# A new opening for a linear-attention and gated-MLP kernel: the first four token tiles are centred before they are transposed, and normalised at the exit of V

## The chip, the cores and the metric

The kernel runs on one core of a Trainium2 chip. Its time is the device time of one execution in microseconds (us), as the median of several runs. A profile is the record of one such execution: every instruction with its engine, start and length, the waits between engines, and the packets of the transfers. The engines are PE (matrix multiply, with PEld for its weight loads), DVE (vector), ACT (activation functions), POOL (general purpose) and SP, which in this kernel does nothing but issue transfers (DMAs).

## The reference

One layer norm of `x` (2048 tokens, 640 features) feeds two branches, whose outputs are added to `x`. Branch A is linear attention with 32 heads of 20 features; its feature map is a softmax of plus and of minus the mapped vector. Branch B is a gated MLP of width 1536.

```
xn  = (x - mean) / sqrt(var + 1e-5)
q, k, v = split(xn @ wqkv)                      # per head: 2048 x 20
phi(a)  = concat(softmax(a @ w_phi), softmax(-(a @ w_phi)))
kv  = sum over s of phi(k)[s, f] * v[s, d];   z = sum over s of phi(k)[s, f]
A   = ((phi(q) @ kv) / (phi(q) . z + 1e-6)) @ wo
B   = (silu(xn @ w1) * (xn @ w3)) @ w2
out = x + A + B
```

All inputs and the output are bfloat16.

## The kernel before

The 2048 tokens are 16 tiles of 128, the 640 features 5 chunks of 128. The kernel is written as a list of operations; a planner inside it (`schedule`, lines 166 to 370) gives each operation a planned start, picks the engine where an operation may run on two, and so fixes the order of the instructions on each engine. `emit` then turns each dependence into a semaphore wait. All engines work through their own lists in order; an instruction that waits holds back everything behind it on its engine. All transfers are issued by SP, in one list. Loads and stores go through line 606, transfers that transpose (called turns here) through line 612. All matmuls but the fillers and the transposes are recorded by line 544, all instructions of DVE, ACT and POOL by line 552, so groups are told apart by their tiles.

What happens in the opening, by its names:

- `load_x` brings tiles of `x` into `x_tok`: tiles 0, 1, 2, 3 alone, then 4 to 7, 8 to 11 and 12 to 15 together. `wv` (the V columns of wqkv) comes in two halves of 320 columns, `phi_s` holds w_phi, `load_wT` turns the K part of wqkv into `wqkT` in five pieces (and later the Q part), `load_w13` brings column ranges of w1 and w3 (512 columns of each at a time).
- `ln_stats` computes mean and variance of a tile on DVE (two statistics and one aggregate) and 1/sqrt(var + eps) on POOL into `mv[:, t, 4]`. `ln_apply` normalises the tile in place, on DVE, or from tile 4 on also on ACT.
- Tiles 0 to 3 are transposed on PE (`xn_transpose`, against `ident`) into `xnT`, the transposed normalised input. Tiles 4 to 15 are turned into `xnT` by a DMA each (`turn`), which SP issues once the tile is normalised.
- `v_half` and `v_tile` multiply a tile of `xnT` by `wv` into `v2`, which keeps a column of ones beside each head. `fold(1, dc)` multiplies `wqkT` by a block diagonal `BDc` of w_phi, so that `Wkp` is w_k times w_phi; `fold(0, dc)` does the same for Q into `Wqp`. `k_tile` multiplies by `Wkp` and takes the exponentials of plus and minus the result (`ekt`); `k_norm` sums and scales them (DVE and POOL).
- `mlp(b, fc)` is one MLP unit: 10 matmuls of 512 tokens (5 by w1, 5 by w3), a tanh on ACT into `th`, two steps on DVE into `t1` and `hT`.
- `filler` gives PE matmuls on zeros in the first 12 planned us where it would be idle.
- `consts_fold` makes the mask `GF` that `block_diag` needs on POOL, `consts_late` the masks `GK`, `PT` and `epsc` and `ones_late` the ones in `v2`.

Then come, with MLP units between them, V and K of tiles 4 to 15, the sum over tokens (`kv_sum`, `kv_back`), Q (`q_proj`), the attention output of each tile (`q_tok`, whose result `o_tok` is turned into `oT`), and the output tiles (`out_tile`: 12 chunks of w2 and 5 of wo, then the sum with `x` from `xres`, and the store).

The planner's main rules that the change touches: a transfer ends 1.35 us after its bytes at 330 GB/s behind those before it; among operations of one engine that can start within 0.03 us of the earliest, the one with the highest level goes first; dependences are kept by regions of 32 bytes (`GRAN`), and an overwrite of what the same engine has read needs no wait, except on POOL.

Of the kernel before, what the change touches and what calls it, by code (L numbers as in the profile page):

```python
# [9 lines left out]
D = 640  # L10
# [10 lines left out]
ENGINES = ("PE", "ACT", "DVE", "POOL", "SP")  # L21
SEM = {"PE": 0.06, "ACT": 0.04, "DVE": 0.04, "POOL": 0.08, "SP": 0.05}
MODE = 0.097
GRAN = 32
BACKLOG = 2.5


# [4 lines left out]
class _Op:  # L32


    __slots__ = ("ways", "eng", "emit", "raw", "war", "bankd", "succ", "unit", "ismm", "start", "end", "inc", "sem",
                 "clock", "idx", "part", "level", "off", "done", "nbytes", "busy", "left", "name", "deps", "gates")

    def __init__(self, ways):
        self.ways = ways
        self.eng = next(iter(ways)) if len(ways) == 1 else None  # L40
        self.raw, self.war, self.bankd, self.succ = set(), set(), set(), []
        self.unit = None
        self.ismm = self.inc = self.part = self.done = False
        self.sem = None
        self.nbytes = 0
        self.level = 0.0
        self.off = 0.0
        self.name = ""
        self.gates = []


class _Unit:
# [11 lines left out]
class _Program:  # L64
# [101 lines left out]
    def schedule(self, start, filler=None, filler_until=0.0):  # L166
# [45 lines left out]
        def commit(o, e, t):  # L212
            nonlocal bus, pool_prev
            o.eng = e
            o.emit, o.busy, dur = o.ways[e]
            o.start = t
            free[e] = t + o.busy
            if o.nbytes:
                bus = max(bus, t + 0.6) + o.nbytes / 330e3
                o.end = bus + 1.35  # L220
            else:
                o.end = t + dur
            o.done = True
# [66 lines left out]
        while left:  # L290
            best = None
            pick = None
            if ready_u:
                t0 = free["PE"]
                blocked = set()
                cands = []
                for u in ready_u:
                    extra = MODE if u.mode != mode else 0.0
                    u.at = max(unit_time(u), t0 + extra)
                for u in sorted(ready_u, key=lambda u: (-u.level, u.mms[0].idx)):  # L300
                    opts = []
                    for k in range(0, 8, u.banks):
                        if blocked & set(range(k, k + u.banks)):
                            continue
                        g = group_time(u, k)
                        if g < 1e8:
                            opts.append((max(g, u.at), fit(k, u.banks, u.at), k))
                    if opts:
                        x = min(opts)
                        if pick is None or x[0] < pick[0] - (0.03 + MODE):  # L310
                            pick = (x[0], u, x[2])
                    if u.banks == 4 and u.at <= t0 + 1.0 and not blocked and (not opts or x[0] > u.at + 0.03):
                        k = min((group_time(u, k, True), k) for k in (0, 4))[1]
                        blocked |= set(range(k, k + 4))
                if pick is not None:
                    best = (pick[0], "PE", pick[1], pick[2])
            for e in ("ACT", "DVE", "POOL", "SP"):
                if not ready[e]:
                    continue
                ts = [(max(free[e], op_time(o, e)), o) for o in ready[e]]  # L320
                t = min(x[0] for x in ts)
                t, o = min((x for x in ts if x[0] <= t + 0.03), key=lambda x: (-x[1].level, x[1].idx))
                if best is None or t < best[0]:
                    best = (t, e, o, None)
            assert best is not None, [(len(ready_u), {e: len(r) for e, r in ready.items()})]
            t, e, x, k = best
            if e == "PE":
# [44 lines left out]
    def emit(self, finish):  # L372
# [55 lines left out]
def bass_parallel_sum__linear_kernel_hedgehog__glu_gated_swiglu__prompt_kernel(  # L428
# [52 lines left out]
    th = new("th", [128, 3, 512], f32)  # L481
    t1 = new("t1", [128, 3, 512], bf)
    xres = new("xres", [128, 4, D], bf)

    RX = region(20480)
    x_tok = new("x_tok", [128, T, D], bf, RX)
# [60 lines left out]
    def way(eng, name, args, kw, busy, lat):  # L547
# [2 lines left out]

        def emit():
            return getattr(e, name)(*[at(a, u) for a in args], **{k: at(v, u) for k, v in kw.items()})  # L552
        return eng, (emit, busy, lat)

    def sb(*aps):
        return [a for a in aps if hasattr(a, "ap")]
# [51 lines left out]
    def turn(o, i, level=0.0, dram=False):  # L608
        n = 2
        for s in o.shape:  # L610
            n *= s
        return P.dma("SP", lambda: nc.sync.dma_start_transpose(o, i), sb(o), sb(i), n,  # L612
                     1.3 * n / 163840, level)

# [13 lines left out]

    def load_wT(which, e, level):
        turn(wqkT[:, which * DC + e:which * DC + e + 1, :],
             A_wqkv[:, which * D + 128 * e:which * D + 128 * e + 128], level)

# [41 lines left out]
    def ln_stats(t0, n, level):  # L676
        for t in range(t0, t0 + n):
# [5 lines left out]
        m, v, r, z = mv[:, t0:t0 + n, 0], mv[:, t0:t0 + n, 1], mv[:, t0:t0 + n, 4], mv[:, t0:t0 + n, 5]  # L683
        add([w_op("POOL", "tensor_scalar_add", (r, v, EPS), 0.21, 0.25)], [r], [v], None, level)
        add([w_op("POOL", "tensor_tensor", (r, r, mhalf[:, 0:n], ALU.pow), 0.55 + 0.1 * (n - 1),
                  0.6 + 0.1 * (n - 1))], [r], [r, mhalf[:, 0:n]], None, level)
# [2 lines left out]
            add([w_op("POOL", "tensor_tensor", (z, z, r, ALU.mult), 0.21, 0.25)], [z], [z, r], None, level)  # L689

    def ln_apply(t, level):
        o, m, s, z = x_tok[:, t, :], mv[:, t, 0:1], mv[:, t, 4:5], mv[:, t, 5:6]
# [3 lines left out]
        add(ways, [o], [o, m, s, z] if t >= 4 else [o, m, s], None, level)  # L696

    def xn_transpose(t, level):
        u = P.begin(1, level)
# [266 lines left out]
    load_w13(0, 512, lv - 20)  # L966
    load_x(8, 12, lv - 21)
    load_w13(512, 1024, lv - 22)
    load_x(12, 16, lv - 23)
# [1 line left out]
    for e in range(DC):  # L971
        load_wT(0, e, lv - 30 - e)

    consts_fold()
    for t in range(4):
        ln_stats(t, 1, 1e5 - t)
        ln_apply(t, 2e5 - t)
    block_diag(0)
    for t in range(4):
        xn_transpose(t, 5e4 - 10 * t + 15)  # L980
    for t in range(4, T, 2):
        ln_stats(t, 2, 1e5 - t)
        ln_apply(t, 2e5 - t)
# [105 lines left out]
```

## Time and profile before

| | us |
|---|---|
| four runs | 278.53, 277.63, 277.31, 278.11 |
| median | 277.87 |
| the profiled execution, its own time | 278.53 |
| its span, from first to last instruction | 276.8 |

The profiled execution is the first of the four; its span leaves out 1.7 us that lie around the instructions. The granted clock of PE was 1.00.

The first 17 us, busy time of each engine (PE's includes 37 matmuls on zeros):

| PE | PEld | DVE | ACT | POOL |
|---|---|---|---|---|
| 13.92 | 8.63 | 8.05 | 6.71 | 10.04 |

A row of the timeline gives start, length, engine, line, operation, tile written and tiles read, shapes and count, and in brackets the idle time before it and what ended it. A length of several instructions runs from the first's start to the last's end, and a matmul's end is some 0.17 us after the next one's start, because they are pipelined: steps between starts are what one costs. A row of the chain of waits gives start, length and what the end of the kernel hung on in that time.

### The profile page before, as it was taken

What the parts mean: (1) busy time and instruction counts of PE and PEld (TensorE: products, weight loads), DVE (VectorE), ACT (ScalarE), POOL (GpSimd) and SP (SyncE); (2) the same over time, 40 slices, a digit from 0 to 9 for tenths busy, and PEclk for the clock granted to TensorE, in tenths of its full rate; (3) what the DMA queues carried; (4) which work ended last, traced back from release to release, by engine and by line L of the source; (5) the groups of instructions that cost most, each with busy time, mean ns of one, the idle gap of its engine ahead of it and who ended that gap; (6) DMA issues with size and microseconds to landing.
All of it is one profiled execution on the core that took longest, in us unless ns stands there. A gap on an engine that the chain in (4) does not pass through costs nothing.

```text
span 276.8 us, 5029 instructions
## 1 busy us (share of the span) xinstructions
PE 268.4 (97%) x2076; PEld 158.9 (57%) x2097; DVE 177.5 (64%) x311; ACT 101.8 (37%) x188; POOL 60.5 (22%) x101
## 2 busy tenths in 40 slices
PE   7899999999999999999999999999999999999996
PEld 3575565666664446644444445767777775444774
DVE  3667899998756444478968979667761215566212
ACT  2478577456445441247573383010000001322000
POOL 7712548999459000000000000000000000000000
PEclk9999999999999999999999999999999999999999
DMA  7899997840000000801211121233332222000001
GB/s 209 130 343 243 247 190 146 153 153 0 2 0 0 2 0 2 266 22 26 46 27 24 24 50 24 73 94 100 96 90 78 73 71 73 0 0 0 26 24 47
DMA packets 40583, 21.98 MB, mean 79 GB/s; under 512 B 26992, under 2 KB 40560, under 8 KB 40560
## 3 DMA queue, kind: packets, MB, share of 16 engines
q1 hardware_dynamic: 40560, 21.66, 32.5%
q8 instruction: 16, 0.26, 0.4%
q14 instruction: 7, 0.06, 0.1%
HBM read 12.81 MB, written 2.62 MB: 56 GB/s over the span
## 4 chain that ended last, share of the span: by engine, by line
PE 85%; DMA 5%; SPq 4%; DVE 2%; ACT 2%; issue 2%; POOL 1%
PE PS L544 85%; SPq L612 3%; DMA xnT<-x_tok 3%; DMA x_tok<-in_A_x_dram 2%; ACT EqT L552 2%; SPq L606 1%; DVE bst L552 1%; POOL mv L552 1%; DVE hT L552 0%; DVE den_s L552 0%; DVE xres L552 0%; ACT e_s L552 0%; DVE x_tok L552 0%; DVE mv L552 0%; DVE pr_s L552 0%
## 5 line engine op out<-in xcount | busy, mean ns | idle before, releaser
L544 PE MATMUL PS<-xnT,w_s 128*128 128x512 bf16 x463 | 105.9, 379 | 1.7 <-issue 0.5
L544 PEld LDWEIGHTS PS<-xnT,w_s 128*128 128x128 bf16 x480 | 46.3, 98 | 54.2 <-DVE hT L552 1.0
L544 PE MATMUL PS<-w_s,hT 128*128 128x320 bf16 x384 | 55.0, 299 | 0.0
L552 ACT ACTIVATE th<-PS 128x512 f32<-128x512 f32 x48 | 28.8, 599 | 64.1 <-PE PS L544 63.9
L552 DVE SCALAR_TENSOR_TENSOR t<-th,PS 128x512 bf16<-128x512 f32 x48 | 32.5, 677 | 22.9 <-ACT th L552 22.9
L544 PEld LDWEIGHTS PS<-w_s,hT 128*128 128x128 bf16 x384 | 37.1, 98 | 14.9
L552 POOL TENSOR_TENSOR ekt<-ekt,rS 128x640 bf16<-128x640 bf16 x32 | 39.6, 1271 | 11.1 <-DVE rS L552 11.1
L552 DVE TENSOR_TENSOR xres<-PS,xres 128x640 bf16<-128x640 f32 (+1 forms) x17 | 13.4, 786 | 41.2 <-PE PS L544 41.2
L552 DVE SCALAR_TENSOR_TENSOR hT<-t,PS 128x512 bf16<-128x512 bf16 x48 | 32.4, 675 | 1.4 <-PE PS L544 0.4
L552 ACT ACTIVATE EqT<-PS 128x512 bf16<-128x512 f32 x40 | 21.7, 594 | 12.5 <-PE PS L544 12.5
L552 DVE TENSOR_REDUCE S<-ekt 128x64 f32<-128x1280 bf16 x16 | 23.3, 1474 | 4.2 <-ACT ekt L552 4.1
L544 PE MATMUL PS<-wv,xnT 128*128 128x320 bf16 x160 | 24.9, 299 | 0.6 <-DMA xnT<-x_tok 0.6
L544 PE MATMUL PS<-wo_s,oT 128*128 128x320 bf16 x160 | 24.5, 299 | 0.0
L552 DVE TENSOR_TENSOR prod<-PS,g_s 128x1280 bf16<-128x1280 f32 x16 | 23.9, 1491 | 0.5
L544 PE MATMUL PS<-Wkp,xnT 128*128 128x320 bf16 x160 | 24.0, 299 | 0.0
L544 PE MATMUL PS<-xnT,Wqp 128*128 128x512 bf16 x96 | 23.1, 380 | 0.3 <-issue 0.2
L552 ACT ACTIVATE ekt<-PS 128x640 bf16<-128x640 f32 x32 | 20.5, 705 | 6.9 <-PE PS L544 6.8
L552 ACT ACTIVATE e_s<-PS 128x64 f32<-128x64 f32 x32 | 9.1, 284 | 37.8 <-PE PS L544 37.3
L544 PEld LDWEIGHTS PS<-wv,xnT 128*128 128x128 bf16 x160 | 15.2, 98 | 8.1 <-DVE hT L552 1.1
L552 DVE BATCH_NORM_STATS2 bst<-x_tok 128x6 f32<-128x320 bf16 x32 | 14.2, 478 | 7.7 <-DMA x_tok<-in_A_x_dram 7.6
L544 PEld LDWEIGHTS PS<-wo_s,oT 128*128 128x128 bf16 x160 | 15.7, 98 | 6.1
L544 PEld LDWEIGHTS PS<-Wkp,xnT 128*128 128x128 bf16 x160 | 15.5, 98 | 6.1 <-DVE hT L552 0.3
(58 smaller groups left out, 150.3 us busy)
## 6 DMA issues: line engine op xcount, KB each, us to landing
w_s<-in_B_w_dram SPq DMA_DIRECT2D x6, 640.0 KB, 9.0
xres<-in_A_x_dram SPq DMA_DIRECT2D x16, 160.0 KB, 2.2
out_dram<-xres SPq DMA_DIRECT2D x15, 160.0 KB, 1.8
x_tok<-in_A_x_dram SPq DMA_DIRECT2D x3, 640.0 KB, 5.8
w_s<-in_B_w_dram SPq DMA_DIRECT2D x1, 1920.0 KB, 9.3
wv<-in_A_wqkv_dram SPq DMA_DIRECT2D x2, 400.0 KB, 4.6
wo_s<-in_A_wo_dram SPq DMA_DIRECT2D x1, 800.0 KB, 6.1
x_tok<-in_A_x_dram SPq DMA_DIRECT2D x4, 160.0 KB, 4.6
```

Of the source, the lines that this page charges most:

```text
L544: return nc.tensor.matmul(o(u.k), l, r, start=start, stop=stop, skip_group_check=shared)
L552: return getattr(e, name)(*[at(a, u) for a in args], **{k: at(v, u) for k, v in kw.items()})
L606: return P.dma(eng, lambda: queue[eng].dma_start(o, i), sb(o), sb(i), n, 0.45, level, after)
L612: return P.dma("SP", lambda: nc.sync.dma_start_transpose(o, i), sb(o), sb(i), n, 1.3 * n / 163840, level)
```

## The change

It has five parts.

1. *The first four tiles.* ACT makes the negative mean of the tile (a copy scaled by -1/640 with an accumulated sum, `junk` takes the copy), DVE or ACT adds it to the tile (`centre`, into `xc`), PE transposes the centred tile (`xc_transpose`, into `xcT`; tile 0 in two parts), and `v_first` computes V from `xcT`, scaling by 1/sqrt(var + eps) as V leaves PSUM. The statistics, the normalisation in place and the transposes into `xnT` are still made for these tiles, since K, Q and the MLP use them; they follow.
2. *Transfers.* Tiles 0, 1 and 2 come first, then `wv` as five pieces of 128 rows, then tile 3, `phi_s`, the first 256 columns of w1 and of w3, the five `wqkT` turns, tiles 4 to 7, the next 256 columns of w1 and w3, and the rest as before.
3. *The planner's figures.* A transfer ends 1.2 us after its bytes, a turn from DRAM 1.0 and one from SBUF 0.2 later; operations can be given an earliest start; `block_diag` is not planned before 8 us, the late masks and ones not before 30.
4. *The planner's choices.* The highest level goes first among operations that can start within 0.09 us; an operation of high level is taken off an engine if another would end it sooner.
5. *Dependences.* Regions of 8 bytes; an overwrite of what the same engine has read now waits for it on all engines but PE.

```diff
-GRAN = 32
+GRAN = 8
...
-                o.end = bus + 1.35
+                o.end = bus + 1.2 + o.extra
...
-            t = 0.0
+            t = o.early
...
-                t = max(t, d.end + SEM[e] if d.eng != e or e == "POOL" or d.nbytes or o.nbytes else d.start)
+                t = max(t, d.end + SEM[e])
...
-                t, o = min((x for x in ts if x[0] <= t + 0.03), key=lambda x: (-x[1].level, x[1].idx))
+                t, o = min((x for x in ts if x[0] <= t + 0.09), key=lambda x: (-x[1].level, x[1].idx))
+                if len(o.ways) > 1 and o.level > 1.5e6:
+                    other = min(max(free[f], op_time(o, f)) + o.ways[f][2] for f in o.ways if f != e)
+                    if other < t + o.ways[e][2] - 0.02:
+                        ready[e].remove(o)
+                        del o.ways[e]
+                        moved = True
+                        continue
...
-                if d.eng == e and e != "POOL" and not d.nbytes and not o.nbytes:
+                if d.eng == e == "PE":
                     continue
...
+    def centre(t, level):
+        o, i, z = xc[:, t, :], x_tok[:, t, :], mv[:, t, 6:7]
+        add([way("ACT", "activation", (junk[:], i, ACT.Copy), dict(scale=-1.0 / D, accum_out=z), 0.8, 0.9)],
+            [junk[:], z], [i], None, level)
+        add([w_op("DVE", "tensor_scalar", (o, i, z, None, ALU.add), 0.35, 0.44), w_act(o, i, ACT.Identity, D, 1.0, z)],
+            [o], [i, z], None, level)
...
+    def xc_transpose(t, level):
+        n = 2 if t == 0 else 1
+        u = P.begin(n, level)
...
+    def v_first(t, level):
+        P.begin(2, level, stream="V").name = f"V{t}"
+        for i in range(DC):
+            for q in range(2):
+                mm(q, lambda k, q=q: bank(k + q, 320), xcT[:, t, i, :], wv[:, i, 320 * q:320 * q + 320],
+                   i == 0, i == DC - 1)
...
+        add([w_act(o, src, ACT.Copy, D, r), w_op("DVE", "tensor_scalar", (o, src, r, None, ALU.mult), 0.74, 0.83)],
+            [v2[:, t, 0:672]], [r], [0, 1], 1e6)
...
     load_x(0, 1, lv)
-    for q in range(2):
-        load(wv[:, :, 320 * q:320 * q + 320], wqkv_t[:, :, 2 * D + 320 * q:2 * D + 320 * q + 320], lv - 2 - 2 * q,
-             )
-        load_x(q + 1, q + 2, lv - 3 - 2 * q)
-    load_x(3, 4, lv - 6)
-    load(phi_s[:], phi_t, lv - 7)
+    load_x(1, 2, lv - 1)
+    load_x(2, 3, lv - 2)
+    for c in range(DC):
+        load(wv[:, c, :], wqkv_t[:, c, 2 * D:3 * D], lv - 3 - c)
+    load_x(3, 4, lv - 8)
+    load(phi_s[:], phi_t, lv - 9)
+    load_w13(0, 256, lv - 10)
     for e in range(DC):
-        load_wT(1, e, lv - 8 - e)
+        load_wT(1, e, lv - 12 - e)
     load_x(4, 8, lv - 19)
-    load_w13(0, 512, lv - 20)
+    load_w13(256, 512, lv - 20)
...
+    up = 2e6
+    for t in range(4):
+        ln_stats(t, 1, 2e5 - 10 * t)
     consts_fold()
+    n = len(P.all)
+    block_diag(0)
+    late(n, 8.0)
     for t in range(4):
-        ln_stats(t, 1, 1e5 - t)
-        ln_apply(t, 2e5 - t)
-    block_diag(0)
+        centre(t, up - t)
+        ln_apply(t, 1e5 - t)
     for t in range(4):
-        xn_transpose(t, 5e4 - 10 * t + 15)
+        xc_transpose(t, 6e4 - 10 * t + 15)
+    for t in range(4):
+        xn_transpose(t, 3e4 - t)
...
     for t in range(4):
-        for q in range(2):
-            v_half(t, q, 5e4 - 10 * t - q)
+        v_first(t, 6e4 - 10 * t)
...
+    n = len(P.all)
     consts_late()
     ones_late()
+    late(n, 30.0)
```

As the planner orders the changed program, PE's list in the opening is: 10 fillers, the transposes of centred tile 0, 4 fillers, those of tile 1, V of tile 0, the transposes of tile 2, V of tile 1, the transposes of tile 3, V of tiles 2 and 3, the four sets of transposes of normalised tiles, one MLP unit, three folds, one MLP unit, two folds, one MLP unit, K of tiles 0 to 3, one MLP unit, then V and K of tiles 4 to 8. SP's list after tiles 4 to 7 is: w1 and w3 (256 columns each), tiles 8 to 11, w1 and w3, tiles 12 to 15, w1, the turns of tiles 4 and 5, w3, one `wqkT` turn, the turns of tiles 6 and 7, one `wqkT` turn, the turns of tiles 8 and 9.

More of the change, by code (lines that the diff above doesn't have):

```diff
@@ L35 @@
     __slots__ = ("ways", "eng", "emit", "raw", "war", "bankd", "succ", "unit", "ismm", "start", "end", "inc", "sem",
-                 "clock", "idx", "part", "level", "off", "done", "nbytes", "busy", "left", "name", "deps", "gates")
+                 "clock", "idx", "part", "level", "off", "done", "nbytes", "busy", "left", "name", "deps", "gates", "early", "extra")
     def __init__(self, ways):
@@ L49, in __init__ @@
         self.gates = []
+        self.early = 0.0
+        self.extra = 0.0
 class _Unit:
@@ L316, in schedule @@
                     best = (pick[0], "PE", pick[1], pick[2])
+            moved = False
             for e in ("ACT", "DVE", "POOL", "SP"):
@@ L321, in schedule @@
                 t = min(x[0] for x in ts)
-                t, o = min((x for x in ts if x[0] <= t + 0.03), key=lambda x: (-x[1].level, x[1].idx))
+                t, o = min((x for x in ts if x[0] <= t + 0.09), key=lambda x: (-x[1].level, x[1].idx))
[6 more added lines that the diff above has]
+                        continue
                 if best is None or t < best[0]:
                     best = (t, e, o, None)
+            if moved:
+                continue
             assert best is not None, [(len(ready_u), {e: len(r) for e, r in ready.items()})]
@@ L483, in bass_parallel_sum__linear_kernel_hedgehog__glu_gated_swiglu__prompt_kernel @@
     xres = new("xres", [128, 4, D], bf)
+    xcT = P.sbuf("xcT", [128, 4, DC, 128], bf, P.base[xres[:].name])
+    xc = P.sbuf("xc", [128, 4, D], bf, P.base[th[:].name])
+    junk = P.sbuf("junk", [128, D], bf, P.base[t1[:].name])
     RX = region(20480)
@@ L552, in emit, with late @@
             return getattr(e, name)(*[at(a, u) for a in args], **{k: at(v, u) for k, v in kw.items()})
+        emit.__name__ = name
         return eng, (emit, busy, lat)
+    def late(first, us):
+        for o in P.all[first:]:
+            o.early = us
     def sb(*aps):
@@ L611, in turn @@
             n *= s
-        return P.dma("SP", lambda: nc.sync.dma_start_transpose(o, i), sb(o), sb(i), n,
-                     1.3 * n / 163840, level)
+        d = P.dma("SP", lambda: nc.sync.dma_start_transpose(o, i), sb(o), sb(i), n, 1.3 * n / 163840, level)
+        d.extra = 1.0 if dram else 0.2
+        return d
     x_t = A_x.rearrange("b (t p) d -> p (b t) d", p=128)
@@ L632, in load_wT @@
         turn(wqkT[:, which * DC + e:which * DC + e + 1, :],
-             A_wqkv[:, which * D + 128 * e:which * D + 128 * e + 128], level)
+             A_wqkv[:, which * D + 128 * e:which * D + 128 * e + 128], level, True)
     zeroed = []
@@ L682, in ln_stats @@
             add([w_op("DVE", "bn_aggr", (o, i), 0.13, 0.21)], [o], [i], None, level)
-        m, v, r, z = mv[:, t0:t0 + n, 0], mv[:, t0:t0 + n, 1], mv[:, t0:t0 + n, 4], mv[:, t0:t0 + n, 5]
+        m, v, r, z = mv[:, t0:t0 + n, 0], mv[:, t0:t0 + n, 1], mv[:, t0:t0 + n, 4], mv[:, t0:t0 + n, 6]
         add([w_op("POOL", "tensor_scalar_add", (r, v, EPS), 0.21, 0.25)], [r], [v], None, level)
@@ L691, in ln_apply @@
     def ln_apply(t, level):
-        o, m, s, z = x_tok[:, t, :], mv[:, t, 0:1], mv[:, t, 4:5], mv[:, t, 5:6]
+        o, m, s, z = x_tok[:, t, :], mv[:, t, 0:1], mv[:, t, 4:5], mv[:, t, 6:7]
         ways = [w_op("DVE", "tensor_scalar", (o, o, m, s, ALU.subtract, ALU.mult), 0.35, 0.44)]
@@ L696, in ln_apply, with emit, src @@
         add(ways, [o], [o, m, s, z] if t >= 4 else [o, m, s], None, level)
+    def centre(t, level):
[7 more added lines that the diff above has]
+        u = P.begin(n, level)
+        u.name = f"cT{t}"
+        for dc in range(DC):
+            l = xc[:, t, 128 * dc:128 * dc + 128]
+            j, b = (0, dc) if n == 1 or dc < 3 else (1, dc - 3)
+            def emit(l=l, j=j, b=b):
+                a = (u.k + j) * 1024 + 128 * b
+                return nc.tensor.transpose(PSb[:, a:a + 128], l, ident[:])
+            P.mm(emit, [l, ident[:]], j, 0.056, 128)
+        for j, a, b in ((0, 0, DC),) if n == 1 else ((0, 0, 3), (1, 3, DC)):
+            def src(k, j=j, n=b - a):
+                return PSb[:, (k + j) * 1024:(k + j) * 1024 + 128 * n].rearrange("p (c n) -> p c n", n=128)
+            o = xcT[:, t, a:b, :]
+            add([w_act(o, src, ACT.Copy, 128 * (b - a)), w_copy(o, src, 128 * (b - a), 2)], [o], [], [j], 1e6)
+    def v_first(t, level):
[4 more added lines that the diff above has]
+                   i == 0, i == DC - 1)
+        o = v2[:, t, 0:672].rearrange("p (b h c) -> p b h c", b=2, c=21)[:, :, :, 0:DH]
+        r = mv[:, t, 4:5]
+        def src(k):
+            return bank2(k, 320).rearrange("p b (h c) -> p b h c", c=DH)
+        add([w_act(o, src, ACT.Copy, D, r), w_op("DVE", "tensor_scalar", (o, src, r, None, ALU.mult), 0.74, 0.83)],
+            [v2[:, t, 0:672]], [r], [0, 1], 1e6)
     def xn_transpose(t, level):
```

## The prediction

> **What bounds the kernel now.** I read the shares of busy time first, then the chain that ended last, then TensorE's (PE's) own waits, then the first 30 us in order of time.
>
> ```profile
> span 276.8 us, 5029 instructions
> ...
> PE 268.4 (97%) x2076; PEld 158.9 (57%) x2097; DVE 177.5 (64%) x311; ACT 101.8 (37%) x188; POOL 60.5 (22%) x101
> ...
> PE 85%; DMA 5%; SPq 4%; DVE 2%; ACT 2%; issue 2%; POOL 1%
> ```
>
> PE is the bound: only what removes PE work or PE waiting counts. The chain in order of time shows where PE is not the bound (start, length, what):
>
> ```profile
> 10.76 1.28 SPq L612
> ...
> 12.08 5.29 DMA x_tok<-in_A_x_dram
> ...
> 17.40 1.67 DVE bst L552 x4
> ...
> 21.08 0.45 DVE x_tok L552
> ...
> 21.55 7.21 DMA xnT<-x_tok
> ...
> 28.90 8.41 PE PS L544 x60
> ```
>
> The end of the kernel hangs on tile 4: SP must first issue everything ahead of the load of tiles 4 to 7 (12.08), these are normalised by 21.53, and the transfer that turns tile 4 lands at 28.76, although it was issued at 21.55: it stood 7.21 us behind loads already queued. From 28.90 on PE runs on almost without idle. PE's timeline around it:
>
> ```profile
> 8.56 0.85 PE L544 MATMUL PS<-wv,xnT 128*128 128x320 bf16 x5
> ...
> 14.05 0.23 PE L544 MATMUL PS<-BDc,wqkT 128*128 128x140 bf16 x1 [0.70 <-DMA wqkT<-in_A_wqkv_dram]
> ...
> 18.37 5.60 PE L544 MATMUL PS<-Wkp,xnT 128*128 128x320 bf16 x40
> ...
> 24.02 4.26 PE L544 MATMUL PS<-xnT,w_s 128*128 128x512 bf16 x19
> ...
> 28.90 1.52 PE L544 MATMUL PS<-wv,xnT 128*128 128x320 bf16 x10 [0.61 <-DMA xnT<-x_tok]
> ```
>
> So the first V starts at 8.56, two MLP units fill 24.02 to 28.3, and V of tile 4 waits 0.61 us. The stretches of the DMA (us, clock, share, GB/s) explain the 7.21:
>
> ```profile
> 14.00:17.00 3.00, 1.00 0.98 340
> 17.00:20.00 3.00, 1.00 1.09 355
> 20.00:23.00 3.00, 1.00 1.09 356
> ...
> 25.50:28.00 2.50, 1.00 0.58 36
> ...
> 35.00:38.40 3.40, 1.00 1.52 61
> ```
>
> Loads stream at 340 to 356 GB/s until about 25.5; then 2.5 us move next to nothing before the turns go through. 35.0 to 38.4 is the same again, the next time turns stand behind loads.
>
> **The yardstick.** In the order of the changed program, four MLP units stand ahead of V of tile 4, not two. A unit is 10 matmuls, 2.16 us (from 42.02 to 44.18 in the timeline). If V of tile 4 starts at 28.90 + 2 x 2.16 = 33.2 us, the end is where it was; each us sooner is a us won, each later one lost. A sooner start of PE is worth nothing beyond that. Two chains decide that start.
>
> **PE's chain.** Tile 0 lands at 2.97 (the first statistics start there). The mean on ACT by accumulation is not in the trace; its nearest rows are 0.70 (a 640-wide copy on ACT) and 0.92 (the ACT form of the normalisation); I take 0.8, centring on DVE 0.45, so transposes from about 4.4. The last of five wv pieces is issued after seven others. Seven issues took 0.81 to 4.28, 0.50 each, so at 4.3; eight pieces are 1.31 MB, and the DMA moved 247 and 325 GB/s in 2 to 4 and 4 to 6 us, so it lands at 6.5 to 7. V of tile 0 ends at about 7.2. Then two transposes (0.29 each, 9.34 to 9.63), three V (1.36 each), four transposes of normalised tiles (1.16) and one MLP unit: 7.2 + 0.6 + 4.1 + 1.2 + 2.2 = 15.3. Before, the fifth wqkT piece was issued at 10.76 and let the fold run at 14.05. Now twelve issues stand ahead of the five turns instead of seven: 2.5 us, so 16.5 (15.3 if the first two turns take 1.27 like the others, not 2.01 and 1.75). Then the rest of the folds (4 x 0.32), two units, four K (18.37 to 24.02, 5.65), one unit: 16.6 + 1.3 + 4.3 + 5.65 + 2.2 = 30.0. The third unit needs the second w1/w3 pair, queued behind tiles 4 to 7, which land at 17.38 + 2.5 = 19.9: two pieces of 0.33 MB at 355 GB/s land at 20.8 and 21.7, against a need at 20.0 and 21.1, so 0.8 us of waiting, up to 2.4 with the lag of w1 and w3 before. PE would be ready for tile 4 at 30.8 to 32.4.
>
> **The DMA's chain.** The load of tiles 4 to 7 goes out at 12.08 + 2.5 = 14.6. Before, 3.93 MB of loads stood between it and the first turn. Now the SP order has tiles 4 to 7, half of one w1/w3 pair, tiles 8 to 11, a whole pair, tiles 12 to 15 and one more w1: 4.59 MB, as the second half of x comes ahead of the turns and half a pair went out early. The extra 0.66 MB costs 1.85 us at 355 GB/s. Half-pairs come in rows of 512 bytes, not 1024; packets that small in a load are not in the trace (640 bytes moved at 325 GB/s against 355), so 0 to 0.4 us, I take 0.2. Turn of tile 4: 28.76 + 2.5 + 1.85 + 0.2 = 33.3. Low end 31.0: the wqkT turns issue at 1.27 (-1.2) and nearly half of the dead 2.5 us is gone (-1.1). High end 34.5: the first two w1/w3 issues meet a full queue and each takes what a w issue took at 14.89 (1.80 against 0.5), nearly all of which I count (+1.2). DVE does not decide: its statistics for tiles 4 and 5 stand behind the third MLP unit's two evictions (0.67 and 0.69), about 26 to 27 for the normalised tile, while the queue is full until 32.
>
> **Sum.** The later chain, 33.3 + 0.14 (28.76 to 28.90) = 33.4, against 33.2: +0.2 us. The profiled execution took 278.53 with a span of 276.8, so 1.7 lie around it; it would become 278.7. The median is 0.66 below that execution, so I predict 278.1.
>
> **What is costed at nothing.** Four more sets of transposes (1.2 us of PE) and the filler taken out: covered by 1 to 2.5 us that PE waits for the turn; without that cover +1.2. DVE gains four centrings (1.8), one V eviction (0.8), copies (1.1), ACT four sums (2.8 to 3.7): they were busy 8.1 and 6.7 of the first 17 us. The gathered GK, PT and epsc masks go behind 30 us on POOL: at most 5 us ahead of the phi_k products, which end at 89.3 where kv needs them at 107.5. Fewer waits of an engine on itself (finer regions): statistics took 0.51 with and 0.42 without, on DVE, which does not bound. Around the q tiles the order of MLP units shifts a little: 0.5 either way, by the 0.5 that PE waited there for hT.
>
> **Two rules against the change.** Row: filler matmuls of 512 columns start 0.425 us apart until about 5.2 us and at half of that and less later, so a fresh PE is slow. The Trainium skill, "TensorE: Matmul & The Clock Gate", Part 1, says that about 3.4 us of little activity set the clock back to half. Fewer fillers and V of tile 0 waiting on pieces leave PE half idle from 4.5 to 7. By the rule the 40 V matmuls could run at 0.27 in place of 0.136 us, an estimate of +5.4 us on PE's chain; by the row, whose granted clock is 1.00 throughout, nothing. Row: the wv halves of 400 KB landed after 4.1 and 5.1 us. The skill's "DMA: Bandwidth & Descriptors", Bandwidth, says to batch to 1 MiB, as 64 KB reach 138 GB/s; five pieces of 160 KB at that rate would land near 11 us, an estimate of +4 on the same chain. Either alone moves that chain to about 35, +1.5 to 2 at the end.
>
> **Rivals.** *The same* (0.37): as above, 277.3 to 278.7. *Faster* (0.30): the turn is not held by the dead stretch and PE's own chain decides, V of tile 4 at 31.0 to 32.2, so -1.0 to -2.2: 275.7 to 276.9. For it: the first turns at 9 us followed loads without such a stretch. Against: both later ones had it. *Slower* (0.33): the turns of tiles 6 and 7 now stand behind another 0.66 MB of w3 and a wqkT turn. Turn 5 at 33.9, w3 +1.85, wqkT 0.5, turn 6 0.6: 36.9, needed at 33.4 + 2 x 2.72 = 38.8. It decides once that passage takes 1.9 us longer; with the 3.4 us of the stretch from 35.0 it is 40.3, a wait of 1.5, +1.7: 279.6 (to 280.2 with the high end of the first turn). For it: that stretch came when turns were queued behind two loads; against: one load alone (34.90) let the next turns through at once. *The opening does not get earlier* (within the others): V of tile 0 at 8.5 again moves PE's chain by 1.3, to 32.1 to 33.7, still about the turn.
>
> **Range.** 0.3% is 0.83 us, about what a measurement of this kernel can tell from no change; the chances above use it. The likeliest case's own range is 277.3 to 278.7; 8 times in 10 I reach into both sides, 275.8 to 280.2.
>
> **What would show it.** First V at 5 to 6 us; a wait for wqkT at about 15 to 16.5; a wait of PE for w at about 20; the load of tiles 4 to 7 issued near 14.6; V of tile 4 near 33.4, released by the turn; little wait at tile 6. It is wrong if V of tile 4 is released by PE's own queue, or starts before 32.4 or after 34.

## The result, and the profile after

| | before | after |
|---|---|---|
| median, us | 277.57 (66 executions) | 277.10 (43 executions) |
| lowest to highest | 276.87 to 278.53 | 276.21 to 277.84 |
| the profiled execution | 278.53 | 276.80 |
| its span | 276.8 | 275.1 |

The ratio is 0.9983, with a 95% interval of 0.9978 to 0.9988: 0.47 us faster. Small, but told apart from no change. The two profiled executions lie 1.7 us apart, more than three times as far, because the one of before is the longest of its 66 (0.96 above its median) and the one of after lies 0.30 below its own. Whatever is read from that pair has to be corrected for this.

The page of the changed kernel, its shares and its chain:

```profile
span 275.1 us, 5036 instructions
...
PE 267.1 (97%) x2072; PEld 159.4 (58%) x2094; DVE 183.3 (67%) x324; ACT 102.0 (37%) x188; POOL 60.7 (22%) x101
...
PE 86%; DVE 4%; ACT 4%; issue 2%; DMA 2%; POOL 0%
```

PE is the bound as before; SP's queue has left the chain, and the shares of DVE and ACT rose from 2% to 4% each. In the opening the chain now runs through the third MLP unit and the statistics of tiles 4 and 5. The chain up to tile 4:

```profile
21.19 1.04 PE PS L559 x4
...
23.49 0.21 DVE mv L567
...
25.30 0.47 DVE x_tok L567 x2
25.77 6.00 DMA xnT<-x_tok
31.77 0.14 issue
31.91 13.74 PE PS L559 x100
```

The turn of tile 4 is issued at 25.77, right after DVE normalised the tile (the prediction expected 26 to 27), and lands 6.00 us later, at 31.77 (expected 33.3). PE's timeline, to be held against that of before:

```profile
6.35 1.90 PE L559 MATMUL PS<-wv,xcT 128*128 128x320 bf16 x10
...
12.76 1.28 PE L766 MATMUL PS<-ident,x_tok 128*128 128x128 bf16 x20
14.85 2.11 PE L559 MATMUL PS<-xnT,w_s 128*128 128x512 bf16 x9 [0.81 <-DVE xnT L567]
16.79 1.11 PE L559 MATMUL PS<-BDc,wqkT 128*128 128x140 bf16 x18
...
21.19 2.13 PE L559 MATMUL PS<-xnT,w_s 128*128 128x512 bf16 x9 [0.50 <-DVE hT L567]
...
31.91 1.52 PE L559 MATMUL PS<-wv,xnT 128*128 128x320 bf16 x10 [0.99 <-DMA xnT<-x_tok]
```

V begins at 6.35 instead of 8.56 (an MLP unit, at 14.85, now precedes the folds), and PE stands ready for tile 4 at 31.91 - 0.99 = 30.92, with four MLP units done instead of two. The turn costs 0.99 on top. The stretches of the transfers:

```profile
23.00:25.50 2.50, 2.50 (x20) 1.74 (x19) 2.29 (x6) 0.78 (x2) 1.33 (x4) 1.00 1.09 349
25.50:28.00 2.50, 2.50 (x20) 1.82 (x19) 2.43 (x9) 2.38 (x4) 0.62 (x3) 1.00 1.09 360
28.00:31.00 3.00, 2.87 (x15) 1.29 (x14) 2.36 (x7) 2.52 (x5) 1.27 (x5) 1.00 1.19 166
```

Each row ends with granted clock, DMA share and GB/s. The last row mixes two things: the loads stream on to about 29 (326 GB/s from 28 to 29), and then comes the lull before the turn, 129 and 43 GB/s in the two us to 31. It is somewhat shorter than in before, where 36 GB/s were left over 2.5 us.

### The profile page after: what moved, and what is told of

The parts are those of the page before. It is cut to its first block, busy times and chain, and to the rows that moved or that the text cites. A ratio compares the mean times of both kernels' runs of the same rounds, so it can differ in the third digit from the quotient of the medians.

```text
span 275.1 us, 5036 instructions
## 1 busy us (share of the span) xinstructions
PE 267.1 (97%) x2072; PEld 159.4 (58%) x2094; DVE 183.3 (67%) x324; ACT 102.0 (37%) x188; POOL 60.7 (22%) x101
## 3 DMA queue, kind: packets, MB, share of 16 engines
q1 hardware_dynamic: 41280, 21.66, 31.7%
## 4 chain that ended last, share of the span: by engine, by line
PE 86%; DVE 4%; ACT 4%; issue 2%; DMA 2%; POOL 0%
PE PS L559 84%; ACT EqT L567 3%; DMA xnT<-x_tok 2%; PE PS L1006 2%; DVE hT L567 1%; DVE t L567 1%; DVE den_s L567 1%; PE PS L736 1%; POOL mv L567 0%; DVE xnT L567 0%; ACT th L567 0%; ACT e_s L567 0%; DVE g_s L567 0%; DVE pr_s L567 0%; DVE xres L567 0%
## 5 line engine op out<-in xcount | busy, mean ns | idle before, releaser
L559 PE MATMUL PS<-wv,xnT 128*128 128x320 bf16 x120 | 18.3, 299 | 1.0 <-DMA xnT<-x_tok 1.0
L559 PEld LDWEIGHTS PS<-wv,xnT 128*128 128x128 bf16 x120 | 11.7, 98 | 7.1 <-issue 1.5
L559 PEld LDWEIGHTS PS<-xnT,Wqp 128*128 128x128 bf16 x100 | 9.3, 98 | 10.8
```

Source lines behind the costliest of these rows:

```text
L559: return nc.tensor.matmul(o(u.k), l, r, start=start, stop=stop, skip_group_check=shared)
```

## The experiments

Each run stood beside executions of the kernel before on the same chip, and the ratio is taken against those. "V4" is the start of V of tile 4 in the run's profile, the wait that of PE just before it, "units" the MLP units ahead of it.

| run | median us | ratio [95%] | span | V4 (wait) | units |
|---|---|---|---|---|---|
| b_again | 277.75 | 1.0002 [0.9994, 1.0011] | 276.2 | 28.40 (none) | 2 |
| a_again | 277.11 | 0.9980 [0.9971, 0.9988] | 275.6 | 32.40 (0.97) | 4 |
| b_transfers | 277.46 | 1.0004 [0.9991, 1.0016] | 276.4 | 30.77 (none) | 3 |
| a_oldtransfers | 276.91 | 0.9970 [0.9961, 0.9980] | 275.2 | 29.84 (0.33) | 3 |
| b_planner | 278.81 | 1.0042 [1.0027, 1.0057] | 277.4 | 28.94 (none) | 2 |
| a_dup3 | 277.37 | 0.9998 [0.9984, 1.0011] | 275.6 | 32.41 (1.25) | 4 |
| a_dup10 | 278.22 | 1.0024 [1.0014, 1.0033] | 276.6 | 33.41 (none) | 4 |
| b_dup3 | 278.26 | 1.0017 [1.0008, 1.0027] | 277.0 | 29.25 (none) | 2 |
| a_hold26 | 279.41 | 1.0055 [1.0033, 1.0077] | 278.1 | 31.05 (2.16) | 3 |
| hold26_b (the same kernel) | 279.08 | 1.0038 [1.0020, 1.0056] | 277.9 | 30.94 (2.24) | 3 |
| h_fill6 | 279.01 | 1.0046 [1.0021, 1.0071] | 277.2 | 31.88 (1.90) | 3 |
| h_zero8 | 278.42 | 1.0030 [1.0017, 1.0043] | 277.1 | 30.81 (filled) | 3 |
| o_hold24 | 277.67 | 0.9999 [0.9986, 1.0011] | 276.1 | 28.14 (1.36) | 2 |
| c1 | 276.96 | 0.9975 [0.9951, 0.9999] | 273.8 | 28.51 (none) | 3 |
| c1_b (the same kernel) | 277.68 | 0.9984 [0.9962, 1.0006] | 274.3 | 28.99 (0.74) | 3 |
| c1_fill13 | 276.96 | 0.9971 [0.9956, 0.9987] | 275.1 | 29.78 (0.96) | 3 |
| c1_zero4 | 276.86 | 0.9963 [0.9943, 0.9982] | 276.3 | 30.96 (0.85) | 3 |
| c1_look (c1, one execution) | 277.06 | | 275.3 | 30.02 (0.57) | 3 |

### Both kernels once more

No edit.

> The kernel before against itself: ratio 1.000. It shows how far one execution differs from another. If the start of V of tile 4 sets the end (theory of the turn), span minus that start stays at 276.8 - 28.90 = 247.9 us within 0.3, whatever the start is. If the executions differ later (another theory), that difference varies too.

> The changed kernel again: ratio 0.998. Theory of the turn: V of tile 4 starts when the turn of tile 4 lands, at 31.5 to 33, and span minus that start is 275.1 - 31.91 = 243.2 within 0.3. Theory of the opening (the time follows PE's first V): the first V at 6.3 and the time 1.5 to 2 us lower in every execution.

The second profile of before is of an execution of 277.88, and it has no wait at tile 4. PE's timeline of it:

```profile
24.08 4.48 PE L544 MATMUL PS<-xnT,w_s 128*128 128x512 bf16 x20
28.40 1.52 PE L544 MATMUL PS<-wv,xnT 128*128 128x320 bf16 x10
```

The turn had landed at 28.01; PE's own queue sets the start. So the 0.61 that the first profile shows for the turn is not there in every execution. An execution's time less its V4 is nearly constant: 278.53 - 28.90 = 249.63 and 277.88 - 28.40 = 249.48 before, 276.80 - 31.91 = 277.29 - 32.40 = 244.89 after. By this (249.48 and 244.89) the median of before, 277.57, has V4 near 28.1, and the median of after, 277.10, near 32.2. The rule holds beyond these two kernels: time less V4, with 2.16 us added for each unit ahead of it, is 253.80 or 253.81 in b_again, b_transfers and b_dup3, which have the old planner, and 253.51 to 253.55 in after, a_again and the nine other profiles that have the new one and lose nothing behind V4 to a turn, to ACT or to a lower clock.

### The parts

b_transfers is the kernel before with the new load order alone:

```diff
-    for q in range(2):
-        load(wv[:, :, 320 * q:320 * q + 320], wqkv_t[:, :, 2 * D + 320 * q:2 * D + 320 * q + 320], lv - 2 - 2 * q,
...
+    for c in range(DC):
+        load(wv[:, c, :], wqkv_t[:, c, 2 * D:3 * D], lv - 3 - c)
+    load_x(3, 4, lv - 8)
+    load(phi_s[:], phi_t, lv - 9)
+    load_w13(0, 256, lv - 10)
```

a_oldtransfers is the kernel after with the same lines taken back. b_planner is the kernel before with parts 3 to 5 of the change alone.

> The kernel before with the changed order of transfers alone (no centred tiles). Three MLP units stand ahead of V of tile 4, so the start that would leave the time unchanged is 28.90 + 2.16 = 31.1. Theory of the turn: 3.94 MB of loads stand before the turn, 0.66 less than in the changed kernel, so it lands near 31.8 - 1.85 = 29.9 and the time falls by about 1 us. Theory of the opening: without centred tiles PE starts no sooner, so no gain, 0 or more.

> The changed kernel with the order of transfers from before (wv in halves, w1 and w3 by 512 columns). Three MLP units stand ahead of V of tile 4: unchanged time at a start of 31.1. Theory of the turn: tiles 4 to 7 are issued at 12.1 as before, with 0.66 MB more before the turn than before, so it lands at 28.8 + 1.85 = 30.6 and the gain is 0.3 us. Theory of the opening: PE has its first V from centred tiles at about 7, and most of the gain stays, 0.5 us or more.

> The kernel before with the planner's part of the change alone (regions of 8 bytes, 0.09 us, the moves between engines, the ends of transfers, the earliest starts); transfers and tiles as before. Theory of the turn: SP's list is the same up to the turn of tile 4, which lands at 28.8, so 0 within 0.3 us. Theory of the planner (finer regions and better choices give the gain later in the kernel): at least 0.4 us of gain, and span minus the start of V of tile 4 falls by as much.

The new load order alone wins nothing: in b_transfers the turn landed at 30.23, but PE's own queue came to V4 only at 30.77. And after is not better for it: without it the ratio is 0.9970, with it 0.9980, intervals that overlap. The planner's part alone loses 1.2 us. With the old load order under both, the new opening is what makes the difference between b_planner (1.0042) and a_oldtransfers (0.9970): 0.7%, 2.0 us. In the two profiles, 2.3 us apart, 1.3 of it lie ahead of V4 (28.94 against 29.84 - 2.16) and 1.0 behind it. In PE's timeline of b_planner one sees what the old opening does under the new planner:

```profile
7.46 0.69 PE L719 MATMUL PS<-ident,x_tok 128*128 128x128 bf16 x5 [2.14 <-DVE x_tok L564]
...
9.64 2.16 PE L556 MATMUL PS<-wv,xnT 128*128 128x320 bf16 x10
```

PE waits 2.14 us for the first normalised tile, and the first ten V matmuls take 2.16 us where they take 1.52 at full pace. This half pace is not in every execution: the profiled one has a granted clock of 0.993, the other six of b_planner 0.999 or 1.00. Its V4, at 28.94, comes 0.5 later than in b_again; 0.8 more is lost in a wait for ACT's exponentials at 44 to 45 us. The centred tile is there sooner (first transposes at 4.53 in after), which removes this wait.

### How much is covered

a_dup3 and a_dup10 repeat the transposes of the normalised tile 3 in the kernel after, 15 and 50 more (0.84 and 2.8 us of PE); b_dup3 adds 15 to the kernel before.

```diff
             P.mm(emit, [l, ident[:]], 0, 0.056, 128)
+            for _ in range(3 if t == 3 else 0):
+                P.mm(emit, [l, ident[:]], 0, 0.0, 128)
```

> The changed kernel with the transposes of normalised tile 3 made four times (15 more, 0.84 us on PE, all engines' order unchanged). Theory of the turn: PE waited 0.99 us for the turn in the profiled execution, so the wait shrinks to 0.2 and the time is that of the changed kernel within 0.2. Theory of the opening: 0.84 us longer, which would be above the kernel before.

> The same with 50 more transposes, 2.8 us on PE. Theory of the turn: 0.99 of it hidden, 1.8 us longer than the changed kernel. Theory of the opening: 2.8 us longer.

> The kernel before with 15 further transposes of tile 3 (15 x 56 ns = 0.84 us of PE) in its opening. Theory one (in the usual execution of the kernel before PE's own chain sets the start of V of tile 4, as in b_again, where it waited for nothing): about +0.7 to +0.84 us, a ratio of 1.0025 to 1.003. Theory two (the reading of the prediction: V of tile 4 waits 0.61 us for its turn): 0.61 of the 0.84 are hidden, +0.23 us, a ratio near 1.001.

Against a_again, 0.84 us cost 0.18% (0.5) and 2.8 us 0.44% (1.2, 1.6 covered): some cover, as the wait for the turn gives, not the full 2.5 of the prediction's high end. The 0.5 is not clear of noise, since the intervals of a_dup3 and a_again overlap; their profiled executions both take 277.29, with V4 at 32.41 and 32.40. In the kernel before 0.84 us cost 0.47, between the two theories, with the full 0.84 outside the interval. That would fit a turn that decides in some executions and PE in others; in the one that was profiled V4 waited for nothing.

### The turn sent ahead of the loads

In a_hold26 the last loads may not be planned before 26 us, so the turns of tiles 4 and 5 pass them; o_hold24 does so at 24 us, with the old load order, and holds back the turns of the Q part too.

```diff
+    n = len(P.all)
     load_x(12, 16, lv - 23)
     load_w13(1024, 1536, lv - 24)
     for e in range(DC):
         load_wT(0, e, lv - 30 - e)
+    for o in P.all[n:]:
+        o.early = 26.0
```

> The changed kernel, with tiles 12 to 15 and the last third of w1 and w3 not planned before 26 us: SP's list then has three wqkT turns and the turns of tiles 4 and 5 ahead of them. Three MLP units ahead of V of tile 4, unchanged time at 31.1. Theory of the turn: 1.31 MB less (3.7 us) and three turns more (1.8) before the turn of tile 4: near 29.9, a gain of 1.2 against the kernel before. Theory of the opening: no difference from the changed kernel, 0.5.

> The kernel after with the transfer order of the kernel before, and with tiles 12 to 15 and the last third of w1 and w3 not planned before 24 us, so that the turns of tiles 4 and 5 go ahead of them and two MLP units stand ahead of V of tile 4. Theory one (the end follows the start of V of tile 4 less 2.16 us per MLP unit ahead of it): PE's chain is ready at 27.6 to 28.0, the turn lands near 28.0 or sooner, the end comes at 251.8 + 28.0 - 4.32 = 275.5: about the same as the kernel after, a ratio of 0.998; if the turn lands by 27.2, 0.996. Theory two (holding the loads brings a wait of PE of 2 us or more, as in a_hold26): 1.003 or above.

Neither gains. In o_hold24 V4 starts at 28.14, as theory one had it, but the span is 276.1 and not 275.5; 0.4 of that is lost at tile 6, whose turn PE waits for. In a_hold26 the turn lands 0.9 to 1.5 us sooner than in the profiles of after, but one MLP unit fewer stands ahead of it, so PE waits 2.16, and V and K of tile 4 then take 2.41 and 2.35 us instead of 1.52. Two runs ask whether the wait makes them slow. h_fill6 puts 30 more transposes of tile 3 into a_hold26. h_zero8 puts 8 idle matmuls directly into the wait:

```diff
         P.begin(2, level, stream="V").name = f"V{t}"
...
+        for _ in range(8 if t == 4 else 0):
+            P.mm(idle, [], 0, 0.0, 512)
+            P.all[-1].raw = set(zeroed)
         proj(t, wv)
```

> The kernel after with the later loads held back as in a_hold26, and 30 further transposes of tile 3 (each of its five done seven times; 30 x 56 ns = 1.68 us of PE) ahead of V of tile 3. Theory one (in a_hold26 the 2.16 us in which PE stood still for the turn of tile 4 made its next matmuls run at half pace: V and K of tile 4 in 2.41 and 2.35 us instead of 1.52): the added work fills that wait to about 0.5 us, V of tile 4 takes 1.5 us again, and although it does more work the kernel is 1.0 to 1.7 us faster than a_hold26: about 278.0, a ratio near 1.001 to the kernel before. Theory two (V and K of tile 4 were slow for another reason, such as their operands or the transfers running beside them): nothing is won, V of tile 4 keeps 2.4 us, and the ratio stays at 1.0055 or above.

> a_hold26 once more, beside h_zero8 on one chip. Theory one (PE stands still for about 2.2 us ahead of V of tile 4, and V and K of tile 4 then run at 0.27 us a matmul): a ratio of 1.004 to 1.007 and executions spread over 2 us, with V of tile 4 in 2.4 us where the wait is over 2.1. Theory two (the 2.41 us were of that one execution): V of tile 4 in 1.52 us and a ratio near 1.000.

> a_hold26 with 8 idle matmuls (128 x 512, on zeros, 0.213 us each = 1.7 us) put on PE directly ahead of V of tile 4, nothing else. Theory one (half pace after the wait): they fill most of the wait of 2.16 us, V and K of tile 4 take 1.52 us, and the kernel gets 1.3 to 1.7 us faster than a_hold26 although it does more: a ratio of 0.999 to 1.001. Theory two (the slow matmuls have another cause): V of tile 4 keeps 2.4 us, the ratio stays at 1.004 or above.

In h_fill6 the turn came later as well (31.7), so that a wait of 1.90 was left; after it V of tile 4 took 1.52. h_zero8 decides it. First V of tile 4 in PE's timeline of hold26_b and the stretches of that run, then the stretches of h_zero8 (after the counts: clock, DMA share, GB/s):

```profile
30.94 2.49 PE L559 MATMUL PS<-wv,xnT 128*128 128x320 bf16 x10 [2.24 <-DMA xnT<-x_tok]
```

```profile
31.00:33.00 2.00, 2.00 (x10) 1.18 (x11) 1.76 (x5) 0.00 (x0) 1.91 (x8) 0.58 0.73 215
33.00:35.50 2.50, 2.50 (x14) 1.54 (x13) 1.50 (x6) 0.71 (x1) 1.98 (x8) 0.65 1.06 352
```

```profile
31.00:33.00 2.00, 2.00 (x17) 1.43 (x16) 1.72 (x6) 0.62 (x1) 1.90 (x8) 1.00 0.75 169
33.00:35.50 2.50, 2.50 (x21) 1.82 (x19) 1.11 (x4) 1.79 (x4) 2.05 (x8) 1.00 1.04 352
```

With the wait left empty the granted clock fell to 0.58 and 0.65; with it filled by matmuls of zeros it stayed at 1.00, and the two stretches hold 38 matmuls instead of 24. V and K of tile 4 run in 1.53 and 1.52 again. In time this is worth little: the median is 0.7 us lower, but the intervals of the two ratios overlap. The granted clock of each execution tells why. In hold26_b it is 0.993 or 0.994 in five of the twelve, which take 279.31 to 280.06; in the other seven it is 0.999 or 1.00, and five of these take 278.01 to 278.29. In h_zero8 it is 1.00 in all twelve, 277.82 to 279.10. The idle matmuls keep the long executions away and save nothing in the rest. PE's timeline of h_zero8 shows why even against the profiled execution of hold26_b it won only 0.8 us, not the 1.3 to 1.7 expected:

```profile
28.98 1.89 PE L834 MATMUL PS<-zero 128*128 128x512 bf16 x8
30.81 1.53 PE L559 MATMUL PS<-wv,xnT 128*128 128x320 bf16 x10
...
39.40 1.52 PE L559 MATMUL PS<-wv,xnT 128*128 128x320 bf16 x10 [0.83 <-DMA xnT<-x_tok]
```

PE now comes to tile 6 ahead of its turn, which stands behind the loads that were let pass, and waits 0.83 there.

### Towards a version that beats both

c1 is a_oldtransfers with wv in one load behind tiles 0 and 1, which saves SP an issue.

```diff
-    for q in range(2):
-        load(wv[:, :, 320 * q:320 * q + 320], wqkv_t[:, :, 2 * D + 320 * q:2 * D + 320 * q + 320], lv - 2 - 2 * q,
-             )
-        load_x(q + 1, q + 2, lv - 3 - 2 * q)
+    load_x(1, 2, lv - 1)
+    load(wv[:], wqkv_t[:, :, 2 * D:3 * D], lv - 2)
+    load_x(2, 3, lv - 3)
```

> The kernel after with the transfer order of the kernel before and wv in one load behind tiles 0 and 1, so one issue of SP fewer. Theory one (every issue of SP that is ahead of tiles 4 to 7 is worth about 0.5 us at V of tile 4, and a_oldtransfers had its turn just in time): the turn of tile 4 lands near 29.2 and V of tile 4 starts near 29.4, about 0.4 us better than a_oldtransfers: a ratio of 0.9955. Theory two (the first V waits longer for the whole of wv than the issue saves): a ratio of 0.997 to 0.999, with V of tile 4 at 29.9 or later.

> c1 once more, beside c1_fill13 on one chip: 275.3 to 278.8 as before, a ratio near 0.9975.

Its best executions take 275.2 to 275.6 us, but they spread to 278.8 and 280.0, and the two series together, 0.9975 and 0.9984, are not better than after. Three runs ask why it spreads. c1_fill13 tells the planner that wv lands 1.3 us later, c1_zero4 puts 4 idle matmuls ahead of the first V as h_zero8 did, c1_look is one more profile.

> c1 with the planner told that wv lands 1.3 us later, so that idle matmuls and the transposes of the normalised tile 0 fill PE's wait for wv. Theory one (in the slow executions of c1 PE's clock falls after that wait): the executions draw together at 275.3 to 276.5, a ratio of 0.993. Theory two (the spread of c1 comes from when the turn of tile 4 lands, which nothing here changes): 275.3 to 278.8 again, a ratio of 0.9975. Theory three (PE waits instead for the normalised tile 0, which DVE has not ready by 6.5 us): V of tile 0 starts at 8 or later and the ratio is 0.999 or above.

> c1 with 4 idle matmuls (128 x 512 on zeros, 0.85 us at full pace) directly ahead of V of tile 0, in PE's wait of 0.43 to 1.14 us for wv; nothing else moves. Theory one (in the slower executions of c1 the first V and what follows run at half pace after that wait): the executions draw together, none above 277.0, a ratio of 0.993 to 0.995. Theory two (the spread comes from the transfers: when wv or the turn of tile 4 lands): 275.3 to 279 again, a ratio of 0.9975 to 0.9985.

> One more profile of c1. If it falls on a slower execution (over 277.3): by theory one V of tile 0 or the matmuls after it stand at 0.27 us a matmul in place of 0.136; by theory two all run at 0.136, and V of tile 4 or a later tile waits 1 us or more for its turn.

The first V of c1_look (277.06 us) and of c1_zero4 (278.01 us), in PE's timeline of each:

```profile
8.16 2.88 PE L559 MATMUL PS<-wv,xcT 128*128 128x320 bf16 x20 [1.58 <-DMA wv<-in_A_wqkv_dram]
```

```profile
8.77 2.89 PE L559 MATMUL PS<-wv,xcT 128*128 128x320 bf16 x20 [0.91 <-DMA wv<-in_A_wqkv_dram]
```

Twenty matmuls in 2.88 us is full pace, after a wait of 1.58, so in these two executions the clock is not the cause. What moves is the landing of wv: at 7.06, 8.02 and 8.73 us in c1, c1_look and c1_zero4, for executions of 275.56, 277.06 and 278.01; V4 follows at 28.51, 30.02 and 30.96, each time 0.14 after the turn has landed (c1_b, 6.75 and 276.06, and c1_fill13, 7.71 and 276.84, are out of step by at most 0.8). That wv moves the turn is read from five profiles that agree, not from an experiment. Why one load of 800 KB lands up to 2 us apart was not found.

The longest executions are another matter. Their granted clock is 0.988 to 0.994 in the three longest of c1 (278.36 to 278.84) and the five longest of c1_b (278.04 to 279.97); it is 0.999 or 1.00 in all the others of the two series, none above 277.71. In the 24 executions of c1_fill13 and c1_zero4, where PE's wait for wv is filled in part, it is never lower than 0.999, and none takes more than 278.03. So both theories hold: the transfers spread the executions from 275.2 to 278, and above that the clock fell, which filling the wait prevents. None of the eight was profiled, so that the clock fell just behind the wait for wv is likely and not shown.

c1_zero4 has the best ratio of all, 0.9963 [0.9943, 0.9982], but a_oldtransfers, at 0.9970 [0.9961, 0.9980] and within 1.0 us from lowest to highest, is the one to use; it is not told apart from after.

## Why the prediction was wrong

It forecast no change that could be measured, +0.2 us with the median at 278.1, and the kernel became 0.47 faster: 0.7 us apart. The median, 277.10, lies between the range of its likeliest case and that of its faster rival, and its own sign of being wrong came up: V4 before 32.4, at 31.91 in after (32.40 in a_again). Its picture was right in the main: the end follows V of tile 4 less 2.16 us for each MLP unit ahead of it, two units are gained, and the start depends on the later of PE's chain and the turn; V4 is released by the turn in both profiles of after. Two terms failed, and a third error nearly cancelled itself.

- *"Around the q tiles the order of MLP units shifts a little: 0.5 either way", costed at nothing.* It was a gain. From the first product with KVc to the first with hT it is 48.83 us in before (48.82 in b_again) and 48.57 in after and a_again. PE's timeline there, of before and of after:

```profile
145.84 1.25 PE L544 MATMUL PS<-xnT,w_s 128*128 128x512 bf16 x5 [0.47 <-DVE hT L552]
```

```profile
144.25 1.25 PE L559 MATMUL PS<-xnT,w_s 128*128 128x512 bf16 x5 [0.28 <-DVE hT L567]
```

  The wait for hT fell from 0.47 to 0.28. In b_planner, with the old opening, the same stretch takes 48.57: these 0.26 us are the planner's. Against b_again all that follows V4 is 249.48 - 244.89 - 4.32 = 0.27 us shorter, so this stretch is nearly all of it. Against the first profile of before it is 0.42, but 0.1 of that belongs to that one execution: from V4 to the first KVc it took 92.81, where b_again took 92.71 and after 88.39 + 4.32.
- *"Twelve issues stand ahead of the five turns instead of seven: 2.5 us", and so the load of tiles 4 to 7 at 14.6 and the turn at 33.3.* SP's timeline, two rows of before and four of after:

```profile
4.28 7.75 SPq L612 DMA_TRANSPOSE wqkT<-in_A_wqkv_dram  x5
...
12.08 0.58 SPq L606 DMA_DIRECT2D x_tok<-in_A_x_dram  x1
```

```profile
6.92 6.78 SPq L632 DMA_TRANSPOSE wqkT<-in_A_wqkv_dram  x5
13.75 0.58 SPq L626 DMA_DIRECT2D x_tok<-in_A_x_dram  x1
...
21.47 1.60 SPq L626 DMA_DIRECT2D w_s<-in_B_w_dram  x1
25.77 3.04 SPq L632 DMA_TRANSPOSE xnT<-x_tok  x2
```

  The five issues cost what was said: the first wqkT turn was issued at 6.92 and 6.66 in the profiles of after, at 4.28 before, 2.4 to 2.6 later. But the first two of those turns took 1.54 + 1.26 and 2.45 + 1.26 us of SP instead of 2.01 + 1.75, so the load went out at 13.75 and 14.40, only 1.7 and 2.2 later than before (12.08 and 12.21). The prediction had this case in its low end and did not take it: 0.3 to 0.8 us. From that issue to the landing it took 18.0 and 17.9 us, against 16.7 and 15.8 before, 1.2 to 2.2 more, where 2.05 was counted: the runs do not contradict that term. With both, the turn landed at 31.77 and 32.27. That it stood behind the loads, and not behind DVE, holds too, although SP had nothing left to issue from 23.1 until DVE had tile 4 ready at 25.77: the last load ahead of the turn landed at 31.20 (31.69 in a_again, 28.19 and 27.44 in the two profiles of before), and the turn each time 0.57 or 0.58 later.
- *The yardstick, "28.90 + 2 x 2.16 = 33.2".* It comes from the longest of 66 executions, which waited 0.61 for its turn; b_again waited for nothing. At the median V4 is near 28.1 and the mark 32.4, 0.8 sooner. But the turn of tile 4 had been worked out from the same execution (28.76; 28.01 in b_again), so this error stood on both sides and nearly cancelled.

Put together: by the medians V4 of after is near 32.2 against a mark of 32.4, -0.2 where +0.2 was forecast, and 0.27 comes off behind it. That the two make up the 0.47 measured is no proof of its own, since both V4 were worked out from the medians; the 0.27 is measured in the profiles. So rather more than half of the net gain lies behind the opening. The centred tiles save 2.0 us against the old opening under the same planner (b_planner to a_oldtransfers), but 1.2 of them are what that planner costs without them.

The other steps: PE's chain was forecast at 30.8 to 32.4 and was ready at 30.92 and 31.43. First V at 6.35 and 5.86, against 5 to 6. The waits for wqkT and for w did not come: PE reached the folds only at 16.79, not at 15.3, and found wqkT there. It waited for the transposed tile (0.81) ahead of the first MLP unit and for hT (0.50) ahead of the third instead. The slower rival, tiles 6 and 7 behind more loads, did not happen in after, which has no wait at tile 6; it is there in h_zero8, at 0.83. The five pieces of wv landed by 7.6 and 8.3, not near 11. The granted clock reads 1.00 throughout in after, as the row said, but it reads so too where PE is still slow at the start: the first three V matmuls stand some 0.26 us apart, and full pace comes at 7.1 us. That cost about 0.4 us on tile 0 (1.90 for ten matmuls), and in b_again the fillers are as slow until 7.1. The 5.4 us weighed by the rule did not come; but the rule is no empty one: b_planner and hold26_b show half pace after a wait.

## What to carry to other kernels

Before you set a mark from a profiled execution, see where it stands among the other executions: here it was 0.96 us above the median, and the wait that it showed at the decisive place is missing in another profile. Work won ahead of a transfer is worth only what the transfer lets through, and where a forecast ends near zero, a term costed at nothing "either way" decides the sign. Where one kernel's executions spread, look at the granted clock of each beside its time: in hold26_b and c1 it set the long ones apart. In a wait of about 2 us idle matmuls kept PE's clock up here; that they are worth more than they cost was seen only against the executions whose clock had fallen.

## What the runs showed of the hardware

After waits of 2.14 (b_planner), 2.16 (a_hold26) and 2.24 us (hold26_b) PE ran at half pace: the granted clock was 0.50 from 7.53, 31.52 and 31.32 us on, each time for 3.41 us, and then 1.00 again. After waits of 1.90 (h_fill6), 1.58 (c1_look) and 1.36 (o_hold24) it stayed at 1.00. The Trainium skill, "TensorE: Matmul & The Clock Gate", Part 1, puts the time of idling that sets the clock back at about 3.4 us; in these runs about 2.1 us were already enough, and 8 idle matmuls of 512 columns prevented it. It does not come in every execution: the clock is below 0.999 in five of twelve of hold26_b, three of eight of a_hold26, one of seven of b_planner and one of eight of h_fill6. Whether the wait was shorter in the others, or fell otherwise, was not seen, so the waits between 1.90 and 2.14 are no measured limit.
